# A chunked scan that feeds a two-layer network: ten scan units ahead of the first network step, six more by twos inside the first steps

## The chip, the core and the metric

The kernel runs on one core of one Trainium2 chip. The metric is device microseconds of that core. TensorE (PE in the profile, with PEld for its weight loads), VectorE (DVE), ScalarE (ACT), GpSimd (POOL) and the queue of transfers (SP) each work through a list of instructions of their own, in order; semaphores tie them together.

## The reference

Attention-like state scan over 4 batches and 8 heads, 768 tokens of 32 values, state of 16 rows, then a network over all 3072 tokens (256 to 2048 to 256, leaky ReLU):

```python
for c in range(nc):                      # chunks of 32 tokens
    xc, Bc, Cc = (x[:, :, sl], B[:, :, sl], C[:, :, sl])
    cum = np.cumsum(log_a[:, :, sl], axis=-1)
    L = np.exp(cum[:, :, :, None] - cum[:, :, None, :]) * causal
    CB = np.einsum('bhin,bhjn->bhij', Cc, Bc)
    y_intra = np.einsum('bhij,bhjd->bhid', CB * L, xc)
    y_inter = np.einsum('bhin,bhnd->bhid', Cc, state) * np.exp(cum)[..., None]
    y[:, :, sl] = y_intra + y_inter
    state = decay_full * state + sum_j(Bc * xc * decay_from_j)
h = y_as_tokens @ w_in                   # 3072 x 2048
out = np.maximum(0.01 * h, h) @ w_out    # 3072 x 256
```

The weights arrive in double precision; the kernel takes them as pairs of 32-bit words.

## The kernel before

**Units.** The scan is cut into 8 chunks of 96 tokens, each with 4 batches: 32 units of 8 heads, numbered 0 to 31 (four units a chunk). The state rides along as 16 extra rows of each tile, so a unit's tiles have 112 rows. A unit goes through these parts. Its *decay* is a tile of 112 x 768 named `lt`: for the early units a matmul of stacked sums (`decay_pe`, line 257, operands `dl` and `dr`, which `decay_load` brings from DRAM in slots) and an exp on ScalarE (`decay_of`, line 268); for units from 16 on, rows loaded by a transfer (`decay_rows`), a subtraction on GpSimd, an exp, a causal select on GpSimd. Its *scores* are eight small matmuls into a PSUM score tile, which VectorE multiplies into `lt` in two halves (`scores`, lines 313 and 318). Its *output* (`unit_out`: `unit_products`, lines 337 and 346, then `unit_halves`) is eight matmuls for the values and eight for the state; ScalarE copies the state (`stage`) and the values (`xh`, the rounded upper part), GpSimd puts the state into the next chunk's tile in four copies (line 373), and VectorE forms the remainder `xl` (line 380, the function `rest`). `pair_block` (line 400 and 412) does this for two units at a time: the outputs of two finished ones and the scores of two new ones share two score tiles.

**Steps.** The network works on 512-token tiles. For tiles 0 to 3 a step is one tile t and one block f of 128 hidden values: `ffn_in` (line 537, six matmuls, the in-half: upper and lower parts of operands, two K halves), two activations on ScalarE (`gh` and, by `ffn_act`, in place), the remainder `gl` on VectorE (`ffn_low`), and three steps later `ffn_out` (line 561, six matmuls, the out-half). `CELLS` orders the 64 steps: each entry is a tile and a range of blocks, and after each cell its output is copied or added into `ob`. Tile 0 needs units 0 to 5, tile 1 units to 10, tile 2 units to 15. Tiles 4 and 5 are done together at the end by another scheme, which nothing here touches.

**Weights.** Each of 16 blocks is decoded to single precision by passes: absolute value on ScalarE, then on VectorE hold, shift, sign and low (lines 433, 439, 446, 453), a cast to the upper part on ScalarE (`wh`, line 459) and the subtraction for the lower part (`wl`, line 466 on VectorE, or line 500 on GpSimd for the blocks in `POOLED`). `decode(n)` records the next n passes; `defer` and `settle` record the ScalarE and GpSimd operations that follow a pass at a later place.

**Order.** Nothing reorders the work: each engine's list is the order in which the program text records it. Before, sixteen units run one by one ahead of the steps (`FIRST_UNITS`), with the first step's in-half inside the last of them; the running sums for the later units (`columns`, `sum_rows`) follow the scores of unit 15, in the same score tile. From step 8 on, `PAIR` says at which step two new units get their scores.

**PSUM.** `ps_c` holds two score tiles, `ps_d` two tiles for decays and outputs ahead of the steps; after these, the banks of `ps_d` become `ps_o` (two output banks) and `ps_h` (two in-half banks). A new tile waits until the last reader of the old one in its place is done.

Of the kernel before, what the change touches and what calls it, by code (L numbers as in the profile page):

```python
# [18 lines left out]
Q = 96  # L19
NC = S // Q  # L20
QE = Q + N
# [16 lines left out]
    (0, 0, 3), (1, 0, 3), (2, 0, 3), (0, 3, 7), (1, 3, 7), (2, 3, 7),  # L38
    (0, 7, 11), (1, 7, 11), (2, 7, 11), (0, 11, 16), (1, 11, 16), (2, 11, 16), (3, 0, 16),
# [21 lines left out]
def scan_ffn(ctx: ExitStack, tc: tile.TileContext, a_l, b_l, c_l, bn_l, x_l, w_l, out_l):  # L61
# [192 lines left out]
    def decay_pe(u, space):  # L254
# [49 lines left out]
    def scores(u, warm=0, sums=False):  # L304
        c, b = divmod(u, NB)
        lt = lts[u].rearrange("p (g h) i -> p g (h i)", h=2)
        for half in range(2):
# [11 lines left out]
            if half and sums:  # L319
                columns(ccol, upto, AF.Copy, sc[:, 0, 2 * Q:])  # L320
                prow = sc[:, 1, 2 * Q:4 * Q].rearrange("p (g i) -> p g i", g=2)
                for g in range(2):
                    sum_rows(prow[:, g], g)
                nc.scalar.copy(crow, prow)
                nc.sync.dma_start(crow_d.rearrange("(g p) i -> p g i", g=2), crow)
# [254 lines left out]
    with tc.tile_pool(name="ps_d", bufs=2, space=PSUM, reuse_waits="tile") as ps_d:  # L580
# [364 lines left out]
```

## Time and profile before

| | |
|---|---|
| median of 3 runs | 332.81 us (332.06 to 333.81) |
| the profiled execution | 333.69 us, its span 332.0 us |
| transfers | 26.29 MB in 11722 packets |
| granted TensorE clock, mean | 0.992 |

In the profile a row of a timeline gives the start, the duration, the engine, the line, the operation with output and inputs, and in brackets the idle time before it with what ended that wait. A row of groups gives count, busy time, mean of one in ns, and the idle time before. Times are from the start of the span.

### The profile page before, as it was taken

What the parts mean: (1) busy time and instruction counts of PE and PEld (TensorE: products, weight loads), DVE (VectorE), ACT (ScalarE), POOL (GpSimd) and SP (SyncE); (2) the same over time, 40 slices, a digit from 0 to 9 for tenths busy, and PEclk for the clock granted to TensorE, in tenths of its full rate; (3) what the DMA queues carried; (4) which work ended last, traced back from release to release, by engine and by line L of the source; (5) the groups of instructions that cost most, each with busy time, mean ns of one, the idle gap of its engine ahead of it and who ended that gap; (6) DMA issues with size and microseconds to landing.
All of it is one profiled execution on the core that took longest, in us unless ns stands there. A gap on an engine that the chain in (4) does not pass through costs nothing.

```text
span 332.0 us, 6283 instructions
## 1 busy us (share of the span) xinstructions
PE 316.9 (95%) x2407; PEld 246.6 (74%) x2407; DVE 217.4 (65%) x351; ACT 182.2 (55%) x354; POOL 124.6 (38%) x214
## 2 busy tenths in 40 slices
PE   8879889899989999999999999999999999999995
PEld 4446567678868887778888878788876787778774
DVE  5879829996897988783432534167367767657651
ACT  4667637755656475644454443466355556555551
POOL 6258821522342444442323550051034565336100
PEclk9999979999999999999999999999999999999999
DMA  6886605393422812042211301000001000000003
GB/s 183 248 225 184 224 12 168 104 233 109 138 74 85 254 63 85 0 149 63 85 64 29 123 0 65 0 0 2 0 0 63 2 0 0 2 0 2 0 2 126
DMA packets 11722, 26.29 MB, mean 79 GB/s; under 512 B 2380, under 2 KB 4652, under 8 KB 11692
## 3 DMA queue, kind: packets, MB, share of 16 engines
q1 hardware_dynamic: 11692, 25.89, 25.5%
q8 instruction: 19, 0.31, 0.4%
q14 instruction: 11, 0.09, 0.1%
HBM read 22.57 MB, written 3.32 MB: 78 GB/s over the span
## 4 chain that ended last, share of the span: by engine, by line
PE 78%; DVE 9%; ACT 3%; issue 3%; ACTq 0%; DVEq 0%
PE op L561 24%; PE hp L537 22%; PE sc L761 9%; PE sc L780 6%; PE op L780 4%; PE hp L761 3%; PE sc L400 2%; PE sc L313 2%; DVE u L841 2%; DVE c L842 2%; PE sc L337 2%; PE pd L337 2%; PE pd L257 1%; DVE w L446 1%; PE pd L537 1%
## 5 line engine op out<-in xcount | busy, mean ns | idle before, releaser
L550 DVE TENSOR_TENSOR gl<-hp,gh 128x512 fp32r<-128x512 f32 x62 | 42.6, 687 | 58.7 <-ACT hp L547 58.5
L544 ACT ACTIVATE gh<-hp 128x512 fp32r<-128x512 f32 x62 | 37.0, 596 | 67.2 <-PE hp L537 67.1
L561 PE MATMUL op<-gh,wh 128*128 128x512 f32 x128 | 50.9, 398 | 2.7 <-DVE ob L575 1.3
L561 PE MATMUL op<-gh,wl 128*128 128x512 f32 x128 | 49.9, 390 | 0.0
L561 PE MATMUL op<-gl,wh 128*128 128x512 f32 x128 | 49.9, 389 | 0.0
L537 PE MATMUL hp<-xh,wh 128*128 128x512 f32 x124 | 48.7, 393 | 0.1
L537 PE MATMUL hp<-xh,wl 128*128 128x512 f32 x124 | 48.3, 389 | 0.0
L537 PE MATMUL hp<-xl,wh 128*128 128x512 f32 x124 | 48.3, 389 | 0.0
L373 POOL COPY xs<-stage 16x64 f32<-16x64 f32 x112 | 28.6, 256 | 42.3 <-ACT stage L370 35.3
L727 POOL TENSOR_TENSOR sl<-s,sh 128x512 fp32r<-128x512 f32 x8 | 10.4, 1298 | 73.1 <-ACT sh L726 73.1
L547 ACT ACTIVATE hp<-hp 128x512 f32<-128x512 f32 x62 | 36.8, 593 | 0.0
L289 POOL TENSOR_SCALAR_AFFINE_SELECT lt<-lt 96x768 f32<-96x768 f32 x16 | 14.6, 915 | 53.5 <-ACT lt L288 47.5
L561 PEld LDWEIGHTS op<-gh,wh 128*128 128x128 f32 x128 | 24.0, 188 | 10.1 <-DVE ob L575 1.7
L280 POOL TENSOR_TENSOR lt<-lt,ccol 112x768 f32<-112x768 f32 x16 | 24.3, 1520 | 13.8 <-DMA lt<-crow_d 9.6
L537 PEld LDWEIGHTS hp<-xh,wh 128*128 128x128 f32 x124 | 23.3, 188 | 6.2 <-DVE gl L550 1.1
L561 PEld LDWEIGHTS op<-gl,wh 128*128 128x128 f32 x128 | 24.0, 188 | 5.1
L561 PEld LDWEIGHTS op<-gh,wl 128*128 128x128 f32 x128 | 24.0, 188 | 4.7
L537 PEld LDWEIGHTS hp<-xl,wh 128*128 128x128 f32 x124 | 23.3, 188 | 4.9
L537 PEld LDWEIGHTS hp<-xh,wl 128*128 128x128 f32 x124 | 23.3, 188 | 4.7
L793 DVE TENSOR_TENSOR gl<-c,gh 128x512 fp32r<-128x512 f32 x24 | 24.4, 1038 | 1.4 <-ACT c L790 1.2
L789 ACT ACTIVATE gh<-c 128x512 fp32r<-128x512 f32 x24 | 15.0, 626 | 14.6 <-DVE c L842 9.1
L412 DVE TENSOR_TENSOR lt<-sc,lt 112x384 f32<-112x384 f32 x32 | 15.6, 548 | 3.3 <-ACT xh L375 1.9
(164 smaller groups left out, 629.2 us busy)
## 6 DMA issues: line engine op xcount, KB each, us to landing
raw<-w_l SPq DMA_DIRECT2D x16, 512.0 KB, 3.6
lt<-crow_d SPq DMA_DIRECT2D x16, 336.0 KB, 4.9
xs<-x_l SPq DMA_DIRECT2D x8, 384.0 KB, 5.2
out_l<-ob SPq DMA_DIRECT2D x12, 256.0 KB, 2.0
bn<-bn_l SPq DMA_DIRECT2D x8, 231.0 KB, 6.2
bt<-b_l SPq DMA_DIRECT2D x8, 224.0 KB, 3.3
cc<-c_l SPq DMA_DIRECT2D x16, 96.0 KB, 3.3
la<-a_l SPq DMA_DIRECT2D x1, 96.0 KB
```

The costliest lines, as they stand in the source:

```text
L280: nc.gpsimd.tensor_tensor(out=lts[u], in0=lts[u], in1=ccol[:, u * NH:(u + 1) * NH].unsqueeze(2).to_broadcast([QE, NH, Q]), op=ALU.subtract,)
L373: nc.gpsimd.tensor_copy(to[:, :, hh], stage[hh * D:hh * D + N])
L412: nc.vector.tensor_tensor(out=heads, in0=spaces[half][:QE, :, 2 * Q * e:2 * Q * (e + 1)], in1=heads, op=ALU.mult,)
L537: nc.tensor.matmul(hp, lhsT=w_half[half][:, f, k * 128:(k + 1) * 128], rhs=x[t][:, k, :], start=(n == 0), stop=(n == 5),)
L544: nc.scalar.activation(ghs[s], hp, AF.Prelu, alpha=0.01)
L547: nc.scalar.activation(hps[s], hps[s], AF.Prelu, alpha=0.01)
L550: nc.vector.tensor_tensor(out=gls[s], in0=hps.pop(s), in1=ghs[s], op=ALU.subtract)
L561: nc.tensor.matmul(op, lhsT=w_half[half][:, f, DM + m * 128:DM + (m + 1) * 128], rhs=x, start=(first and i == 0), stop=(last and i == 2),)
L761: nc.tensor.matmul(bank, lhsT=w[h], rhs=x[g], start=start and i == 0, stop=i == 2, skip_group_check=True,)
L780: nc.tensor.matmul(outs[t][m], lhsT=w_half[half][:, f, DM + m * 128:DM + (m + 1) * 128], rhs=x, start=first and i == 0, stop=last and i == 2,)
L789: nc.scalar.activation(gh, h, AF.Prelu, alpha=0.01)
L793: nc.vector.tensor_tensor(out=gl, in0=g, in1=gh, op=ALU.subtract)
```

## The change

`FIRST_UNITS` goes from 16 to 10. In the last of these ten, after the decay of unit 11, the scores of units 10 and 11 are taken together, then the first step's in-half, then unit 9's output. Step 0 takes the outputs of 10 and 11 with the scores of 12 and 13, step 2 the outputs of 12 and 13 with the scores of 14 and 15, step 4 the outputs of 14 and 15. The decays of units 12 to 15 use the stacked operands, one in a spare PSUM tile right behind the pair, the other after the next step's in-half; the multiplications of the two units stand in the following step, one on each side of that step's `ffn_low`. The running sums go into the spare tile in step 2. The spare tile holds the output banks' place until step 3; outputs of steps 0 and 1 follow in step 4. The cells have 2, 4 and 4 blocks at first. Blocks 0 to 3 instead of 1 and 2 are subtracted on GpSimd. The decode passes ahead of the steps are spread differently, the absolute value of a block follows the low pass of the one before it, a slot copy moves up, and two transfers (x of the third chunk, weight block 2) are issued later.

```diff
--- before.py
+++ after.py
@@ -35,23 +35,27 @@
 CELLS = (
-    (0, 0, 3), (1, 0, 3), (2, 0, 3), (0, 3, 7), (1, 3, 7), (2, 3, 7),
-    (0, 7, 11), (1, 7, 11), (2, 7, 11), (0, 11, 16), (1, 11, 16), (2, 11, 16), (3, 0, 16),
+    (0, 0, 2), (1, 0, 4), (2, 0, 4), (0, 2, 7), (1, 4, 8), (2, 4, 8),
+    (0, 7, 12), (1, 8, 12), (2, 8, 12), (0, 12, 16), (1, 12, 16), (2, 12, 16), (3, 0, 16),
 )
...
-FIRST_UNITS = 16
-POOLED = (1, 2)
-AHEAD = 2
+FIRST_UNITS = 10
+STACKED = 16
+POOLED = (0, 1, 2, 3)
...
-PAIR = {16: 8, 18: 14, 20: 20, 22: 26, 24: 32, 26: 38, 28: 44, 30: 49}
+STACKED_AT = {12: 0, 14: 2}
+STACKED_OUT = 4
+SUMS_AT = 2
+HELD_OUT = 3
+PAIR = {16: 10, 18: 15, 20: 20, 22: 26, 24: 32, 26: 38, 28: 44, 30: 49}
...
-PASSES = (3, 3)
+PASSES = 2
...
-            if half and sums:
-                columns(ccol, upto, AF.Copy, sc[:, 0, 2 * Q:])
...
+    def late_sums(space):
+        pcol = space[:QE, 0, :ncols]
+        prow = space[:, 1, :2 * Q].rearrange("p (g i) -> p g i", g=2)
+        nc.tensor.matmul(pcol, lhsT=upto, rhs=la, start=True, stop=True)
+        for g in range(2):
+            sum_rows(prow[:, g], g)
+        nc.scalar.copy(ccol, pcol)
+        nc.scalar.copy(crow, prow)
+        nc.sync.dma_start(crow_d.rearrange("(g p) i -> p g i", g=2), crow)
...
-        for half in range(2):
-            for e, u in enumerate(new):
-                lt = lts[u].rearrange("p (g h) i -> p g (h i)", h=2)
+
+        def mults(e):
+            lt = lts[new[e]].rearrange("p (g h) i -> p g (h i)", h=2)
+            for half in range(2):
...
+        return rests, mults
+
+    def pair_now(done, new):
+        rests, mults = pair_block(done, new)
+        for e in range(len(new)):
+            mults(e)
         for rest in rests:
             rest()
...
     def do_sign(f):
         decode_sign(f)
-        defer(decode_abs, f + 1)
...
         defer(decode_high, f)
+        defer(decode_abs, f + 1)
...
         fill_slots(1, SLOTS // 2)
+        fill_slots(SLOTS // 2, SLOTS)
...
         fetch_w(1)
-        fetch_x(2)
         scores(0)
...
         for u in range(FIRST_UNITS):
-            if u == FIRST_UNITS - 1:
-                settle()
-                leads.close()
-                pg = ctx.enter_context(tc.tile_pool(name="pg", bufs=LAG + 2))
-                pob = ctx.enter_context(tc.tile_pool(name="pob", bufs=3))
-                ffn_in(0, free_tile()[:, 0])
-                ffn_act(0)
-                ffn_low(0)
...
             if u + 1 < FIRST_UNITS:
-                scores(u + 1, int(0 < u < 4), u + 2 == FIRST_UNITS)
+                scores(u + 1, int(0 < u < 4))
+            else:
+                pair_now((), (u + 1, u + 2))
+                settle()
+                pg = ctx.enter_context(tc.tile_pool(name="pg", bufs=LAG + 2))
+                ffn_in(0, free_tile()[:, 0])
...
+            if u == 3:
+                fetch_x(2)
+            if u == 4:
+                fetch_w(2)
...
-            if u == 0:
-                decode(2)
-                fill_slots(SLOTS // 2, SLOTS)
             if u:
                 settle(late=True)
-            if u > 1 and u < 11:
-                decode(1)
-        ffn_in(1, score_tile()[:, 0])
-
-    ps_o = ctx.enter_context(tc.tile_pool(name="ps_o", bufs=2, space=PSUM, reuse_waits="tile"))
+                if u != 3:
+                    decode(1)
+        ffn_act(0)
+        ffn_low(0)
+
     ps_h = ctx.enter_context(tc.tile_pool(name="ps_h", bufs=2, space=PSUM, reuse_waits="tile"))
+    spaces = ctx.enter_context(ExitStack())
+    ps_x = spaces.enter_context(tc.tile_pool(name="ps_x", bufs=1, space=PSUM, reuse_waits="tile"))
+    ps_o = None
+
+    def open_outs_pool():
+        nonlocal ps_o, pob
+        spaces.close()
+        leads.close()
...
+    def spare_tile():
+        return ps_x.tile([128, 2, TS], F32, name="px_")
...
     for s in range(total):
...
-        if s >= AHEAD:
+        if s:
             ffn_in(s)
+        if late:
+            decay_pe(late[0], spare_tile())
+        if s == SUMS_AT:
+            late_sums(spare_tile())
         if s:
             ffn_act(s)
         settle()
+        if late:
+            late[1](0)
         if s:
             ffn_low(s)
+        if late:
+            late[1](1)
+        late = None
+        if s in stacked_at:
+            u = stacked_at[s]
+            rests, mults = pair_block((u - 2, u - 1), (u, u + 1))
+            decay_pe(u, spare_tile())
+            for rest in rests:
+                rest()
+            late = (u + 1, mults)
         if s in pair_at:
-            pair_block(*pair_at[s])
-        decode(n)
+            pair_now(*pair_at[s])
+        decode(PASSES)
...
-        if rested or not outs_due or steps[outs_due[0]] not in firsts or outs_due[0] == 0:
+        if s == HELD_OUT:
+            open_outs_pool()
+        elif rested or not outs_due or steps[outs_due[0]] not in firsts or outs_due[0] == 0:
```

On ScalarE, ahead of the steps, from the exp of unit 4 on (`lt` exp, `stage` and `xh` copies; `w32` is a weight block's absolute value, `wh` its upper part). Before:

```order
L268 ACTIVATE lt_307<-pd_304 112x768
L370 COPY stage_335<-pd_318 128x64
L375 CAST xh_237<-pd_318 128x2x96
L428 ACTIVATE w32_350<-raw_203 128x512
L459 CAST wh_150<-w32_194 128x512
L268 ACTIVATE lt_357<-pd_354 112x768
L370 COPY stage_387<-pd_370 128x64
L375 CAST xh_237<-pd_370 128x2x96
L268 ACTIVATE lt_401<-pd_398 112x768
```

With the change:

```order
L272 ACTIVATE lt_305<-pd_302 112x768
L377 COPY stage_333<-pd_316 128x64
L382 CAST xh_237<-pd_316 128x2x96
L272 ACTIVATE lt_350<-pd_347 112x768
L377 COPY stage_380<-pd_363 128x64
L382 CAST xh_237<-pd_363 128x2x96
L272 ACTIVATE lt_394<-pd_391 112x768
L377 COPY stage_421<-pd_404 128x64
L382 CAST xh_237<-pd_404 128x2x96
L472 CAST wh_150<-w32_195 128x512
L441 ACTIVATE w32_435<-raw_204 128x512
L272 ACTIVATE lt_441<-pd_438 112x768
```

The absolute value of block 1 and the cast of block 0 moved from ahead of the exp of unit 5 (`lt_357`) to behind the exp of unit 6 and the copies of unit 4.

On VectorE, the last unit ahead of the steps and steps 0 and 1 (L322 and L420 multiply scores into `lt`, L387 forms `xl`, L563 `gl`, the others are decode passes). Before, from the multiplication of unit 15:

```order
L318 TENSOR_TENSOR lt_792<-sc_827,lt_792 112x384
L318 TENSOR_TENSOR lt_792<-sc_831,lt_792 112x384
L380 TENSOR_TENSOR xl_688<-pd_841,xh_687 128x2x96
L550 TENSOR_TENSOR gl_881<-pd_873,gh_880 128x512
L380 TENSOR_TENSOR xl_688<-pd_885,xh_687 128x2x96
L433 TENSOR_SCALAR w32_747<-w32_747 128x512
L439 TENSOR_SCALAR w32_747<-w32_747 128x512
L446 SCALAR_TENSOR_TENSOR w32_747<-raw_611,w32_747 128x512
L550 TENSOR_TENSOR gl_918<-sc_910,gh_917 128x512
L453 SCALAR_TENSOR_TENSOR w32_747<-raw_611,w32_747 128x512
L433 TENSOR_SCALAR w32_931<-w32_931 128x512
```

With the change, from the low part of unit 11:

```order
L387 TENSOR_TENSOR xl_726<-sc_684,xh_725 128x2x96
L459 SCALAR_TENSOR_TENSOR w32_610<-raw_431,w32_610 128x512
L466 SCALAR_TENSOR_TENSOR w32_610<-raw_431,w32_610 128x512
L420 TENSOR_TENSOR lt_745<-sc_683,lt_745 112x384
L420 TENSOR_TENSOR lt_745<-sc_684,lt_745 112x384
L563 TENSOR_TENSOR gl_768<-hp_760,gh_767 128x512
L420 TENSOR_TENSOR lt_773<-sc_683,lt_773 112x384
L420 TENSOR_TENSOR lt_773<-sc_684,lt_773 112x384
L446 TENSOR_SCALAR w32_778<-w32_778 128x512
L452 TENSOR_SCALAR w32_778<-w32_778 128x512
```

Where before the low parts of steps were separated by decode passes only, the multiplications of units 12 and 13 now stand around the low part of step 1.

On TensorE, from behind the scores of units 14 and 15 at the end of step 2 into step 3, with the change (`px_` is the spare tile, `hp` the in-half's bank):

```order
L261 LDWEIGHTS dl_125
L261 MATMUL px__864<-dr_126,dl_125 112x384
L261 LDWEIGHTS dl_125
L261 MATMUL px__864<-dr_126,dl_125 112x384
L550 MATMUL hp_875<-xh_468,wh_150 128x512
L550 MATMUL hp_875<-xh_468,wl_151 128x512
L550 MATMUL hp_875<-xl_469,wh_150 128x512
L550 MATMUL hp_875<-xh_468,wh_150 128x512
L550 MATMUL hp_875<-xh_468,wl_151 128x512
L550 MATMUL hp_875<-xl_469,wh_150 128x512
L261 LDWEIGHTS dl_125
L261 MATMUL px__885<-dr_126,dl_125 112x384
```

The two decays stand on either side of an in-half, each in the spare tile; before, no decay stands between steps at this place.

More of the change, by code (lines that the diff above doesn't have):

```diff
@@ L262, in decay_pe @@
         after_u = u + SLOTS - LOAD + 1
-        if (u - DIRECT + 1) % LOAD == 0 and after_u < FIRST_UNITS:
-            decay_load(after_u, min(LOAD, FIRST_UNITS - after_u))
+        if (u - DIRECT + 1) % LOAD == 0 and after_u < STACKED:
+            decay_load(after_u, min(LOAD, STACKED - after_u))
     def decay_of(u, space):
@@ L300, in state_decay, with scores @@
         )
-    def scores(u, warm=0, sums=False):
+    def scores(u, warm=0):
         c, b = divmod(u, NB)
@@ L318, in scores @@
             nc.vector.tensor_tensor(out=heads, in0=sc[:QE, :, :2 * Q], in1=heads, op=ALU.mult)
-            if half and sums:
-                columns(ccol, upto, AF.Copy, sc[:, 0, 2 * Q:])
[L321 to L325, printed above, removed]
+    def late_sums(space):
[7 more added lines that the diff above has]
+        nc.sync.dma_start(crow_d.rearrange("(g p) i -> p g i", g=2), crow)
     xh, xl, x32 = {}, {}, {}
@@ L624, in scan_ffn @@
         for u in range(FIRST_UNITS):
-            if u == FIRST_UNITS - 1:
-                settle()
-                leads.close()
-                pg = ctx.enter_context(tc.tile_pool(name="pg", bufs=LAG + 2))
-                pob = ctx.enter_context(tc.tile_pool(name="pob", bufs=3))
-                ffn_in(0, free_tile()[:, 0])
-                ffn_act(0)
-                ffn_low(0)
             v = u + 2
-            if 0 < u and v < FIRST_UNITS:
+            if u:
                 decay_pe(v, free_tile())
@@ L645, in scan_ffn @@
                 decay_pe(v, pd)
-            rest()
             c, b = divmod(u, NB)
-            if c + 2 <= FIRST_UNITS // NB:
+            if c + 2 <= 3:
                 if b == 0 and c:
@@ L653, in scan_ffn @@
                     fetch_bc(c + 2)
-                    if c == 0:
-                        fetch_w(2)
                 if b == 3:
                     fetch_bn(c + 2)
-            if b == 2 and c + 1 < FIRST_UNITS // NB:
+            if u == 3:
+                fetch_x(2)
+            if u == 4:
+                fetch_w(2)
+            if b == 2 and c < 2:
                 state_decay(c + 1)
@@ L661, in scan_ffn @@
                 fetch_more()
-            if u == 0:
-                decode(2)
-                fill_slots(SLOTS // 2, SLOTS)
             if u:
                 settle(late=True)
-            if u > 1 and u < 11:
-                decode(1)
-        ffn_in(1, score_tile()[:, 0])
-    ps_o = ctx.enter_context(tc.tile_pool(name="ps_o", bufs=2, space=PSUM, reuse_waits="tile"))
+                if u != 3:
+                    decode(1)
+        ffn_act(0)
+        ffn_low(0)
     ps_h = ctx.enter_context(tc.tile_pool(name="ps_h", bufs=2, space=PSUM, reuse_waits="tile"))
+    spaces = ctx.enter_context(ExitStack())
[5 more added lines that the diff above has]
+        leads.close()
+        pob = ctx.enter_context(tc.tile_pool(name="pob", bufs=3))
+        ps_o = ctx.enter_context(
+            tc.tile_pool(name="ps_o", bufs=2, space=PSUM, reuse_waits="tile")
+        )
+    def spare_tile():
+        return ps_x.tile([128, 2, TS], F32, name="px_")
     early = {}
@@ L687, in scan_ffn @@
     pair_at[LAST_OUT] = ((NU - 2, NU - 1), ())
-    for c in range(FIRST_UNITS // NB, NC):
+    pair_at[STACKED_OUT] = ((STACKED - 2, STACKED - 1), ())
+    at(early, 0, state_decay, 3)
+    at(early, 1, alloc_x, 4)
+    at(early, 1, fetch_x, 4)
+    at(early, 1, fetch_bc, 4)
+    at(early, 2, fetch_bn, 4)
+    for c in range(STACKED // NB, NC):
         b = PAIR[NB * c]
-        if NB * c > FIRST_UNITS:
+        if NB * c > STACKED:
             b0 = PAIR[NB * (c - 1)]
@@ L867, in scan_ffn @@
     combining, rhs = None, {}
-    outs_due, rested = collections.deque(), False
+    outs_due, rested, late = collections.deque(), False, None
+    stacked_at = {s: u for u, s in STACKED_AT.items()}
     for s in range(total):
```

5 lines of the change are left out of this document (3 added, 2 removed).

## The prediction

> **What bounds the kernel now.** I read the page first, then busy time by stretch, then the timelines of the engines in the stretch that the change rewrites. The profiled execution took 333.69 us, its span 332.0, so 1.69 lie around the span; the median of the runs shown is 332.81, 0.88 below the profiled one.
>
> ```profile
> PE 316.9 (95%) x2407; PEld 246.6 (74%) x2407; DVE 217.4 (65%) x351; ACT 182.2 (55%) x354; POOL 124.6 (38%) x214
> 0.00:30.19 30.19, 26.03 (x417) 15.35 (x417) 22.73 (x56) 18.59 (x40) 16.59 (x47) 1.00 0.72 206
> 30.19:59.49 29.30, 26.62 (x341) 19.22 (x341) 20.80 (x42) 17.67 (x43) 13.76 (x37) 0.94 0.47 151
> 59.49:332.00 272.51, 264.30 (x1651) 212.06 (x1649) 173.90 (x255) 145.93 (x274) 94.26 (x130) 1.00 0.19 57
> ```
>
> After the page's first line the columns are the stretch, its length, then busy time of PE, PEld, DVE, ACT and POOL, the granted clock, the DMA share and GB/s. From 59.49 us on, PE is busy in 264.3 of 272.5 us, and only less matmul work or fewer waits help there. Ahead of it PE is called busy too, but the timeline shows short matmuls that wait for the other engines:
>
> ```profile
> 20.73 0.48 PE L257 MATMUL pd<-dr,dl 123*112 123x384 bf16 x2 [2.01 <-ACT lt L268]
> 30.19 0.86 PE L313 MATMUL sc<-cc,bt 32*112 32x192 f32 x8
> 30.98 0.54 PE L337 MATMUL pd<-lt,xs 112*32 112x96 f32 x16
> 31.57 0.53 PE L257 MATMUL pd<-dr,dl 123*112 123x384 bf16 x2
> 32.03 0.59 PE L313 MATMUL sc<-cc,bt 32*112 32x192 f32 x8
> 42.12 0.69 PE L209 MATMUL sc<-la,upto 96*112 96x256 f32 x2 [0.98 <-DVE lt L318]
> 43.28 0.85 PE L213 MATMUL sc<-upto,la 96*128 96x96 f32 x4 [0.47 <-ACT ccol L210]
> 45.08 0.80 PE L537 MATMUL pd<-xh,wh 128*128 128x512 f32 x1
> 59.49 0.39 PE L537 MATMUL hp<-xh,wh 128*128 128x512 f32 x1
> ```
>
> The scores of unit 10 start at 30.19, those of unit 11 at 32.03: 1.84 us per unit. The first step's matmuls start at 45.08. By 59.49 PE has done the in-halves of six steps and the out-halves of three: nine half steps. So 30.19 to 59.49, 29.30 us, holds the scores of units 10 to 15, the outputs of units 9 to 15, the running sums and nine half steps.
>
> Later, where units go by twos between steps, the chain of waits prices the same work:
>
> ```profile
> 84.08 1.36 PE hp L537 x6
> 86.48 0.86 PE sc L400 x16
> 87.35 1.58 PE op L561 x6
> ```
>
> A half step is 1.36. The first pieces leave 85.44 to 86.48 for the products of two units, 1.04, then 0.86 for the scores of two; the next half step takes 0.22 more than usual. That is 1.90 for two units plus 0.22, against 2 x 1.84 for two units ahead of the steps.
>
> **The lead, units 0 to 9.** Two things move here. The weight block's second half of decoding (ACT's absolute value and cast) leaves its place before the decay of unit 5:
>
> ```profile
> 18.79 0.66 ACT L428 ACTIVATE w<-raw 128x512 f32<-128x512 f32 x1 [1.36 <-DMA raw<-w_l]
> 19.36 0.60 ACT L459 CAST wh<-w 128x512 fp32r<-128x512 f32 x1
> 19.86 0.81 ACT L268 ACTIVATE lt<-pd 112x768 f32<-112x768 f32 x1
> 8.94 1.02 DVE L318 TENSOR_TENSOR lt<-sc,lt 112x384 f32<-112x384 f32 x2 [1.13 <-ACT lt L268]
> 12.48 0.68 DVE L446 SCALAR_TENSOR_TENSOR w<-raw,w 128x512 uint32<-128x512 uint32 x1
> 13.20 0.69 DVE L453 SCALAR_TENSOR_TENSOR w<-raw,w 128x512 uint32<-128x512 uint32 x1
> 13.81 0.95 DVE L183 COPY dr<-dr 120x3072 bf16<-120x3072 bf16 x1
> ```
>
> ACT stood 1.36 us for the raw block, then did both operations, and only at 19.86 the exp for which PE waited 2.01 us at 20.73. In the change both stand two exps later; the block has landed by then (18.79 in this trace, with one more transfer of 384 KB around it), so the 2.01 go. The slot copy of 0.95 moves into DVE's gap of 1.13 before 8.94, where it is hidden; at its old place, 13.81, the multiplication of unit 2 followed it. The two decode operations ahead of it (12.48 and 13.20) return one unit later each, so not all of this is won; I take 0.4 of the 0.95. **Lead: 2.4**, with ends at 1.36 (the DMA wait alone) and 3.0 (2.01 and 0.95). The moved transfer of x for the third chunk, now issued at unit 3 rather than at unit 0, needs to land by unit 8's products some 8 us later; POOL's new subtraction for weight block 0 stands before unit 5's state copies, which are first read four units on.
>
> **The stretch from unit 10 to the ninth half step.** On PE the change needs: nine half steps, 9 x 1.36 = 12.24; three pairs of scores, 3 x 0.86 = 2.58; three pairs of products, 3 x 1.04 = 3.12; unit 9's output, 31.57 - 30.98 = 0.59; four decays (12 to 15) at 32.03 - 31.57 = 0.46, 1.84; the sums, 0.69 + 0.85 = 1.54; three slower restarts, 0.66. Sum 22.57. (It has seven in-halves and two out-halves where the kernel before has six and three, by the hold-back of outputs until step 4.)
>
> Then the waits. Products of a pair write into a score tile, which is free once DVE has multiplied both earlier units' scores out of it. The second unit's multiplications now stand behind a decode pass pair, the first unit's and the step's low half:
>
> ```profile
> L318 DVE TENSOR_TENSOR lt<-sc,lt 112x384 f32<-112x384 f32 x32 | 16.2, 547 | 1.7 <-ACT lt L268 1.1 <-PE sc L313 0.5
> L550 DVE TENSOR_TENSOR gl<-hp,gh 128x512 fp32r<-128x512 f32 x62 | 42.6, 687 | 58.7 <-ACT hp L547 58.5
> L446 DVE SCALAR_TENSOR_TENSOR w<-raw,w 128x512 uint32<-128x512 uint32 x16 | 12.6, 785 | 0.0
> L453 DVE SCALAR_TENSOR_TENSOR w<-raw,w 128x512 uint32<-128x512 uint32 x16 | 15.8, 990 | 0.2
> L380 DVE TENSOR_TENSOR xl<-pd,xh 128x192 fp32r<-128x192 f32 x14 | 4.9, 352 | 5.3 <-ACT xh L375 5.2
> L375 ACT CAST xh<-pd 128x192 fp32r<-128x192 f32 x14 | 4.6, 326 | 0.0
> L370 ACT COPY stage<-pd 128x64 f32<-128x64 f32 x16 | 3.4, 212 | 7.6 <-PE pd L346 7.2 <-POOL xs L373 0.3
> ```
>
> Let P be the end of a pair's scores on PE. ACT's two copies of the first unit, 0.21 + 0.33 = 0.54, let DVE start. Steps 0 to 2: DVE then has three low pieces (3 x 0.35 = 1.05), sign and low passes (0.79 + 0.99), two multiplications (1.02, the pair at 8.94), the low half (0.69), two more (1.02): 5.56, done at P + 6.1. PE meanwhile has decay, in-half, decay, in-half, sums: 0.46 + 1.36 + 0.46 + 1.36 + 1.54 = 5.18, and some 0.3 for the spare tile, whose next writer waits for its last reader. PE waits about 0.6. Steps 2 to 4 have no sums, 3.64 on PE, against 0.7 + 1.78 + 1.02 + 0.69 + 1.02 = 5.21 on DVE, done at P + 5.75: PE waits about 2.1 before the products of units 14 and 15. With 0.1 before the first pair, the waits are 2.8 and the stretch 25.4. **Gain 29.3 - 25.4 = 3.9.** What is queued behind that wait on PE is the out-halves of steps 0 and 1, held for it anyway, and in-half 5. If DVE's passes took 0.68 each as at 12.48 and 13.20, each wait would lose 0.4 and the gain be 4.7; with no wait at all 6.7, which DVE's work excludes. The other end is contention with POOL:
>
> ```profile
> 60.87 2.80 DVE L453 SCALAR_TENSOR_TENSOR w<-raw,w 128x512 uint32<-128x512 uint32 x1
> 60.81 0.87 POOL L289 TENSOR_SCALAR_AFFINE_SELECT lt<-lt 96x768 f32<-96x768 f32 x1 [1.72 <-ACT lt L288]
> 61.65 1.47 POOL L280 TENSOR_TENSOR lt<-lt,ccol 112x768 f32<-112x768 f32 x1
> 64.33 0.50 PE L561 MATMUL op<-gh,wh 128*128 128x512 f32 x1 [1.27 <-DVE ob L575]
> ...
> 25.00 0.69 DVE L446 SCALAR_TENSOR_TENSOR w<-raw,w 128x512 uint32<-128x512 uint32 x1
> 24.36 1.42 POOL L373 COPY xs<-stage 16x64 f32<-16x64 f32 x4 [0.15 <-ACT stage L370]
> ```
>
> A pass of 0.69 took 2.80 while POOL ran two operations of 2.34 together: 2.1 lost. Once in each of the two DVE chains, 4.2, and the gain of 3.9 is gone. I keep the means, which hold the contention of an average pass, because POOL's work in these steps is mostly state copies, four per unit, and beside those a pass took its usual 0.69 (25.00).
>
> [...]
>
> **The first change of cells.** [...] In the change the first copies stand in step 4, ahead of the first pair by decay rows (step 10, POOL's work from step 7), with two in-halves to cover them. That wait goes, but the next cell ends in step 8, amid POOL's work; I take half, **0.6**, ends 0 and 1.27.
>
> The decode count stays 16 blocks; every block is finished before the step that needs it, and PE, at 264.3 of 272.5, remains the bound behind. The number of cells is unchanged, so the output additions are too.
>
> **Sum.** 2.4 + 3.9 + 0.6 = 6.9: 333.69 - 6.9 = 326.8 for an execution like the profiled one, 325.9 against the median.
>
> **Rivals.** *POOL's lock in both chains.* For it: the 2.80 above. Against: the 0.69 beside state copies. Price 4.2: 325.9 + 4.2 = 330.1.
>
> *The clock falls again.*
>
> ```profile
> 41.00:42.00 1.00, 0.14 (x2) 0.00 (x0) 1.00 (x3) 0.00 (x0) 0.85 (x4) 1.00 0.00 0
> 42.00:43.00 1.00, 0.69 (x2) 0.27 (x2) 0.07 (x1) 0.16 (x1) 0.37 (x2) 1.00 0.00 0
> 44.00:45.00 1.00, 1.00 (x33) 0.94 (x32) 0.00 (x0) 0.32 (x1) 0.00 (x0) 0.50 0.00 0
> 46.00:47.00 1.00, 1.00 (x4) 0.71 (x4) 0.09 (x1) 0.00 (x0) 0.51 (x3) 0.50 0.00 0
> ```
>
> Two thinly used microseconds, then half clock for some three, costing about 1.5 of the 29.30. My sum has full clock. A wait of 2.1 before units 14 and 15 may bring this back: 325.9 + 1.5 = 327.4. Against: PE was empty for 2.01 at 20.73 and kept its clock. [...]
>
> *No difference.* The lead is set by data: x of the third chunk or the second weight block lands late at its new place and PE stands at unit 8 or 10 for what the lead gains (2.4), and the lock takes its 4.2 as well: 325.9 + 6.6 = 332.5.
>
> *Slower.* The spare tile is one buffer, used five times in steps 0 to 3 and each time written only after its last reader; PE runs in order, so in-halves queue behind it. I count 0.3. An exp (0.81) behind both a step's activation and a cast (0.60 each) would cost 2.0 each time, 10 in all: 325.9 + 9.7 = 335.6. It decides from (6.9 + 0.3) / 5 = 1.4 per use. Against: the in-half of 1.36 lies between a tile's exp and its next writer.
>
> **How the numbers follow.** The forecast has 0.60, the clock 0.12, the lock 0.15, no difference 0.08, slower 0.05. Best ends, 3.0 + 4.7 + 1.27 = 9.0, give 332.8 - 9.0 = 323.8; I go to 323, since PE's 8.2 idle us behind 59.49 (272.51 - 264.30) may shrink a little as well. The upper end is the lock's with 0.4 for an unlucky lead, 330.5. About 0.5%, 1.7 us, can be told from no change. Faster by more (under 331.1): the forecast, the clock and most of the lock's, 0.86; within: 0.09; slower: 0.05.
>
> **What would show it.** The first in-half about 16 us earlier, near 29; no wait for the raw block before unit 5's exp; PE waits of some 0.6 and 2.1 before the products of units 12/13 and 14/15; the ninth half step ended near 53.2; later stretches the same length as before within a microsecond. Wrong if PE waits in step 1 or 3 for the spare tile by over 1 us, if DVE passes of 2 us stand in steps 0 to 4, or if what is gained by 60 us is lost by 130.

## The result and the profile after

The changed kernel took 323.78 us (median of four executions, 323.30 to 324.69), the kernel before 333.11 beside it: ratio 0.9726, 95% interval 0.969 to 0.9762. That is 9.3 us faster; the forecast was 6.9. Beside the later experiments, on two chips, the kernel before took 334.8 to 334.9 and the changed one 324.14 (ratio 0.9729, 0.9651 to 0.9808) and 324.29 (0.9698, 0.966 to 0.9735). The profiled execution took 324.14, its span 322.4 (332.0 before). First the page's line of engines, then busy time by stretch, cut where the prediction cut it:

```profile
PE 311.1 (96%) x2407; PEld 244.9 (76%) x2407; DVE 213.4 (66%) x349; ACT 181.4 (56%) x354; POOL 132.5 (41%) x216
0.00:27.57 27.57, 25.16 (x418) 14.91 (x418) 21.79 (x54) 17.83 (x38) 18.28 (x48) 1.00 0.74 224
27.57:51.60 24.03, 22.01 (x342) 17.86 (x341) 19.15 (x41) 17.26 (x43) 17.44 (x39) 1.00 0.59 187
51.60:322.40 270.80, 263.88 (x1651) 212.18 (x1649) 172.49 (x256) 146.33 (x275) 96.81 (x130) 1.00 0.18 58
```

The lead ends 30.19 - 27.57 = 2.62 us earlier. The stretch from unit 10 to the ninth half step takes 24.03 instead of 29.30, 5.27 less, at a granted clock of 1.00 where it had 0.94. What lies behind takes 1.71 less. The three make the 9.6 us between the spans.

PE's timeline in the new stretch (one row of each group; the multiplications are waited for in brackets):

```profile
21.62 0.48 PE L261 MATMUL pd<-dr,dl 123*112 123x384 bf16 x2 [0.76 <-ACT lt L272]
...
27.57 1.37 PE L407 MATMUL sc<-cc,bt 32*112 32x192 f32 x16
28.86 0.50 PE L550 MATMUL pd<-xh,wh 128*128 128x512 f32 x1
30.45 0.54 PE L344 MATMUL pd<-lt,xs 112*32 112x96 f32 x16
31.95 0.93 PE L407 MATMUL sc<-cc,bt 32*112 32x192 f32 x16
33.05 0.48 PE L261 MATMUL px__742<-dr,dl 123*112 123x384 bf16 x2 [0.17 <-DVE gl L563]
33.24 0.53 PE L550 MATMUL hp<-xh,wh 128*128 128x512 f32 x1
34.75 0.49 PE L261 MATMUL px__770<-dr,dl 123*112 123x384 bf16 x2
34.94 0.53 PE L550 MATMUL hp<-xh,wh 128*128 128x512 f32 x1
36.46 0.60 PE L327 MATMUL px__799<-la,upto 96*112 96x256 f32 x2
36.90 0.58 PE L217 MATMUL px__799<-upto,la 96*128 96x96 f32 x4
37.97 0.54 PE L344 MATMUL sc<-lt,xs 112*32 112x96 f32 x16 [0.50 <-DVE lt L420]
...
44.86 0.54 PE L344 MATMUL sc<-lt,xs 112*32 112x96 f32 x16 [1.36 <-DVE lt L420]
46.01 0.50 PE L574 MATMUL op<-gh,wh 128*128 128x512 f32 x1
51.60 0.39 PE L574 MATMUL op<-gh,wh 128*128 128x512 f32 x1
```

The first in-half starts at 28.86, the ninth half step ends at 51.60. PE waits three times: 0.17 for the spare tile, then 0.50 and 1.36 for the multiplications of the pair before. VectorE's rows around the longer wait:

```profile
41.06 0.68 DVE L459 SCALAR_TENSOR_TENSOR w<-raw,w 128x512 uint32<-128x512 uint32 x1
41.78 0.69 DVE L466 SCALAR_TENSOR_TENSOR w<-raw,w 128x512 uint32<-128x512 uint32 x1
42.39 1.01 DVE L420 TENSOR_TENSOR lt<-sc,lt 112x384 f32<-112x384 f32 x2
43.65 0.69 DVE L563 TENSOR_TENSOR gl<-hp,gh 128x512 fp32r<-128x512 f32 x1 [0.24 <-ACT hp L560]
44.26 1.01 DVE L420 TENSOR_TENSOR lt<-sc,lt 112x384 f32<-112x384 f32 x2
```

It is the chain that the prediction laid out, in its order; the sign and low passes take 0.68 and 0.69.

### The profile page after: what moved, and what is told of

Read it like the earlier page. It is cut to its first block, busy times and chain, and to the rows that moved or that the text cites. A ratio compares the mean times of both kernels' runs of the same rounds, so it can differ in the third digit from the quotient of the medians.

```text
span 322.4 us, 6284 instructions
## 1 busy us (share of the span) xinstructions
PE 311.1 (96%) x2407; PEld 244.9 (76%) x2407; DVE 213.4 (66%) x349; ACT 181.4 (56%) x354; POOL 132.5 (41%) x216
## 4 chain that ended last, share of the span: by engine, by line
PE 83%; DVE 8%; ACT 3%; issue 3%; DMA 2%; SPq 0%; ACTq 0%
PE op L574 26%; PE hp L550 24%; PE sc L792 9%; PE sc L811 6%; PE op L811 4%; PE hp L792 3%; PE sc L407 3%; PE sc L344 3%; DVE c L873 2%; DVE u L872 2%; PE sc L317 1%; PE pd L344 1%; PE pd L261 1%; DMA raw<-w_l 1%; DVE gl L563 1%
## 5 line engine op out<-in xcount | busy, mean ns | idle before, releaser
L563 DVE TENSOR_TENSOR gl<-hp,gh 128x512 fp32r<-128x512 f32 x63 | 43.4, 689 | 58.6 <-ACT hp L560 58.3
L550 PE MATMUL hp<-xh,wh 128*128 128x512 f32 x126 | 49.8, 395 | 0.4 <-DVE gl L563 0.4
L550 PE MATMUL hp<-xh,wl 128*128 128x512 f32 x126 | 49.1, 389 | 0.0
L550 PE MATMUL hp<-xl,wh 128*128 128x512 f32 x126 | 49.0, 389 | 0.0
L380 POOL COPY xs<-stage 16x64 f32<-16x64 f32 x112 | 31.6, 282 | 31.4 <-ACT stage L377 26.9
L284 POOL TENSOR_TENSOR lt<-lt,ccol 112x768 f32<-112x768 f32 x16 | 25.9, 1620 | 3.4 <-DMA lt<-crow_d 2.7
L420 DVE TENSOR_TENSOR lt<-sc,lt 112x384 f32<-112x384 f32 x44 | 21.6, 549 | 3.0 <-ACT xh L382 1.9
```

The source lines that it names most:

```text
L284: nc.gpsimd.tensor_tensor(out=lts[u], in0=lts[u], in1=ccol[:, u * NH:(u + 1) * NH].unsqueeze(2).to_broadcast([QE, NH, Q]), op=ALU.subtract,)
L380: nc.gpsimd.tensor_copy(to[:, :, hh], stage[hh * D:hh * D + N])
L420: nc.vector.tensor_tensor(out=heads, in0=spaces[half][:QE, :, 2 * Q * e:2 * Q * (e + 1)], in1=heads, op=ALU.mult,)
L550: nc.tensor.matmul(hp, lhsT=w_half[half][:, f, k * 128:(k + 1) * 128], rhs=x[t][:, k, :], start=(n == 0), stop=(n == 5),)
L563: nc.vector.tensor_tensor(out=gls[s], in0=hps.pop(s), in1=ghs[s], op=ALU.subtract)
```

## The experiments

The question that the result leaves is which part brought what: the sum of three independent gains (lead, stretch, cells) gave 6.9, and a right total says nothing of its parts.

### The new lead alone

The kernel before with the lead's new order; sixteen units, cells and sums as they were.

```diff
         decode_sign(f)
-        defer(decode_abs, f + 1)
...
         defer(decode_high, f)
+        defer(decode_abs, f + 1)
...
         fill_slots(1, SLOTS // 2)
+        fill_slots(SLOTS // 2, SLOTS)
...
         fetch_w(1)
-        fetch_x(2)
...
+            if u == 3:
+                fetch_x(2)
+            if u == 4:
+                fetch_w(2)
...
-            if u > 1 and u < 11:
-                decode(1)
+                if u != 3 and u < 13:
+                    decode(1)
```

> The kernel before with the new lead alone: slot copy early, absolute value of a block behind the low pass of the one before, passes spread as in the change, x of the third chunk and weight block 2 issued later; sixteen units still run ahead, block subtractions and cells are the old ones. Theory (the terms add): the exp of unit 5 no longer waits behind the raw block, the scores of unit 10 start near 27.6 instead of 30.19, the time falls by 2.6 to about 330.5. Rival (the lead's gain is given back at the sums or at the first step, because the end of the lead waits for something else): 333, no difference.

Measured 334.22 beside 334.76, ratio 0.9982 (0.9946 to 1.0017): no difference. In the profiled execution the units carry the 2.2 us as far as the sums, and some of it is gone behind them:

```profile
27.95 1.05 PE L313 MATMUL sc<-cc,bt 32*112 32x192 f32 x8
36.40 1.04 PE L313 MATMUL sc<-cc,bt 32*112 32x192 f32 x8 [0.88 <-DVE lt L318]
38.21 1.04 PE L313 MATMUL sc<-cc,bt 32*112 32x192 f32 x8 [0.17 <-DVE lt L318]
40.00 1.20 PE L209 MATMUL sc<-la,upto 96*112 96x256 f32 x2 [0.75 <-DVE lt L318]
41.67 1.17 PE L213 MATMUL sc<-upto,la 96*128 96x96 f32 x4 [0.47 <-ACT ccol L210]
43.78 0.80 PE L537 MATMUL pd<-xh,wh 128*128 128x512 f32 x1
58.52 0.39 PE L537 MATMUL hp<-xh,wh 128*128 128x512 f32 x1
```

Unit 10 starts at 27.95 instead of 30.19, the sums at 40.00 instead of 42.12. On the way PE waits 0.88, 0.17 and 0.75 for the multiplications (0.98 in all before); the kernel before has a wait of 0.95 at 33.96 instead, for nothing that its profile shows. Then the sums take 1.20 and 1.17 instead of 0.69 and 0.85: the granted clock was 0.50 from 40 to 46 us, about twice as long as in the kernel before. The first in-half is 1.30 us earlier than before, the end of the ninth half step, at 58.52, still 0.97. Over ten executions even this is not seen in the time; why is not shown.

### The running sums alone

The kernel before with the sums in step 2, in a score tile.

```diff
...
-                scores(u + 1, int(0 < u < 4), u + 2 == FIRST_UNITS)
+                scores(u + 1, int(0 < u < 4))
...
+        if s == 2:
+            late_sums(score_tile())
```

> The kernel before with the running sums alone moved, from behind the scores of unit 15 to step 2, in a score tile. Theory: in the trace of before the sums with their waits keep TensorE from 41.1 to 44.06, and the half clock from 44 to 47 follows from these thin microseconds; moved, they cost 1.0, the clock stays full, and the time falls by about 3.3 to 329.8. Rival (the clock falls anyway, the units' chain sets the end of the lead): at most the two waits of 0.98 and 0.47, with 1.0 added later, about 332.5.

Measured 330.96, ratio 0.9876 (0.9813 to 0.9938): 4.1 us by the ratio, where the theory had 3.3. At their old place the sums had two waits, 0.98 and 0.47, and in the profiled execution stood on the edge of the half clock (1.00 in the window from 42 us, 0.83 in the one from 43, 0.50 in the one from 44); in step 2 they take 0.59 and 0.58 without a wait. The other half of the theory did not come: the clock did not stay full. The four executions have mean clocks of 0.983 to 0.999, and the profiled one stood at half clock for 6.8 us from 21.6 on, behind a wait of 1.9 for the exp of unit 5. What makes up the rest of the 4.1 is open.

### Lead and sums together: as run, the sums alone again

Both edits above were to stand in one kernel. The kernel that ran holds the edit of the sums only; its lead is the old one, and it is the kernel of the section before, line for line:

```diff
...
-                scores(u + 1, int(0 < u < 4), u + 2 == FIRST_UNITS)
+                scores(u + 1, int(0 < u < 4))
...
+        if s == 2:
+            late_sums(score_tile())
```

> The kernel before with two parts of the change: the new order of the lead and the running sums moved out of the last lead unit into step 2. Theory: the lead's 2.6 us were given back only because the running sums at the end of the lead ran in order behind thin work at half clock; with the sums elsewhere the two gains add up, 2.6 + 4.1 = 6.7, about 328. Rival: the lead's gain is lost in any case while units 10 to 15 stand ahead of the steps, since VectorE's multiplications set their pace (waits of 0.88 before units 13 to 15 were seen); then it stays at 331, as with the sums alone.

Measured 329.79 beside 334.89, ratio 0.9883 (0.9813 to 0.9953), on another chip than the 0.9876. That is one kernel measured twice. The wait for the exp of unit 5, which the new lead takes away, stands in its profile:

```profile
21.00 0.48 PE L257 MATMUL pd<-dr,dl 123*112 123x384 bf16 x2 [2.25 <-ACT lt L268]
```

So neither the theory nor the rival was tested: no run here has sixteen units, the moved sums and the new lead.

### The change without its lead

```diff
         decode_sign(f)
+        defer(decode_abs, f + 1)
...
         defer(decode_high, f)
-        defer(decode_abs, f + 1)
...
         fill_slots(1, SLOTS // 2)
-        fill_slots(SLOTS // 2, SLOTS)
...
         fetch_w(1)
+        fetch_x(2)
...
-                if u != 3:
-                    decode(1)
+            if 1 < u < 8:
+                decode(1)
```

> The changed kernel with the old lead: slot copy, passes, absolute value and the two transfers in their old places; ten units ahead, pairs, cells and GpSimd's four subtractions as changed. Theory (the terms add): the scores of units 10 and 11 start near 30.2 instead of 27.57, the rest keeps its length, the time rises by 2.6 to about 326.4. Rival (the pairs in the steps have slack that hides a late lead): 324, no difference.

Measured 327.82, ratio 0.9773 (0.9722 to 0.9824): some 3.5 us more than the changed kernel's 324.29 (measured on the same chip in a later comparison, with the kernel before within 0.2 us of the same time). Here the lead counts. PE's wait for the exp of unit 5 is back, and the first pair starts 30.93 - 27.57 = 3.36 us later:

```profile
20.41 0.48 PE L261 MATMUL pd<-dr,dl 123*112 123x384 bf16 x2 [1.70 <-ACT lt L272]
30.93 0.97 PE L407 MATMUL sc<-cc,bt 32*112 32x192 f32 x16
```

Behind that wait half clock stood for 3.4 us from 21.8 on, and the four executions have mean clocks of 0.987 to 0.995, the changed kernel's 0.997 or more. So a part of the 3.5 us is half clock, and not the order of the lead by itself.

### The change without its cells

```diff
-    (0, 0, 2), (1, 0, 4), (2, 0, 4), (0, 2, 7), (1, 4, 8), (2, 4, 8),
-    (0, 7, 12), (1, 8, 12), (2, 8, 12), (0, 12, 16), (1, 12, 16), (2, 12, 16), (3, 0, 16),
+    (0, 0, 3), (1, 0, 3), (2, 0, 3), (0, 3, 7), (1, 3, 7), (2, 3, 7),
+    (0, 7, 11), (1, 7, 11), (2, 7, 11), (0, 11, 16), (1, 11, 16), (2, 11, 16), (3, 0, 16),
```

> The changed kernel with the cells of before (three blocks in each of the first three cells). Theory: step 2 now wants block 2, whose lower part is done at 38.68 in the trace of the change, while the in-half of step 2 starts at 34.94; TensorE waits up to 3.7, of which the later waits of 0.50 and 1.36 take back some; the time rises by 2 to 3.7, about 326.5. Rival (the cells make no difference, the decode has slack): 324.

Measured 331.09, ratio 0.9894 (0.9857 to 0.993): 6.8 us over the changed kernel's 324.29, twice what was expected, and no better than the sums alone. PE's longest waits in the steps, beside the 1.36 for the multiplications:

```profile
38.17 0.49 PE L550 MATMUL hp<-xh,wh 128*128 128x512 f32 x1 [2.07 <-ACT wh L472]
39.58 0.50 PE L550 MATMUL hp<-xh,wl 128*128 128x512 f32 x1 [0.92 <-POOL wl L512]
76.01 0.50 PE L550 MATMUL hp<-xh,wl 128*128 128x512 f32 x1 [1.23 <-DVE wl L479]
93.56 0.47 PE L574 MATMUL op<-gh,wh 128*128 128x512 f32 x1 [1.74 <-ACT w L441]
```

Three of the four are for decoded weights: the upper part of block 2 (2.07) and its lower part (0.92), both in step 2, and a later lower part (1.23). With cells of 3 blocks step 2 is tile 0 with block 2; with a first cell of 2 it is tile 1 with block 0, decoded long before, and block 2 is wanted at step 4. After the two waits in step 2 half clock stood for 3.4 us from 40.5 on.

### The cells without the units by twos

The kernel of the two sections on the sums (sixteen units, sums moved, the old lead, not the new one that the expectation speaks of) with the cells of the change.

```diff
-    (0, 0, 3), (1, 0, 3), (2, 0, 3), (0, 3, 7), (1, 3, 7), (2, 3, 7),
-    (0, 7, 11), (1, 7, 11), (2, 7, 11), (0, 11, 16), (1, 11, 16), (2, 11, 16), (3, 0, 16),
+    (0, 0, 2), (1, 0, 4), (2, 0, 4), (0, 2, 7), (1, 4, 8), (2, 4, 8),
+    (0, 7, 12), (1, 8, 12), (2, 8, 12), (0, 12, 16), (1, 12, 16), (2, 12, 16), (3, 0, 16),
```

> The kernel before with the new lead, the sums in step 2 and the cells of the change; units 10 to 15 still stand ahead of the steps. Theory: the cells are worth 6 to 7 us only where the units by twos push the decoding of weight blocks into the steps, because cells of 2, 4 blocks ask for block 2 at step 4 instead of step 2; here the blocks were decoded ahead of the steps, so the cells bring nothing but the wait of 1.27 us for the first output copy: 328 to 330. Rival: the cells bring their 6 us whatever the units do, and the units by twos nothing: 323 to 324.

Measured 332.43 beside 334.88, ratio 0.9931 (0.989 to 0.9971): no gain over 0.9876 and 0.9883 without the cells, if anything a loss. The rival's 323 to 324 did not come, though the test was made with the old lead. The kernels with the sums moved make a table; the rows with ten units hold the change's other edits in the steps too:

| ratio to the kernel before | cells of 3, 3, 3 | cells of 2, 4, 4 |
|---|---|---|
| sixteen units ahead, one by one, old lead | 0.9876, 0.9883 | 0.9931 |
| ten ahead, six by twos in steps, old lead | not run | 0.9773 |
| ten ahead, six by twos in steps, new lead | 0.9894 | 0.9698 |

Beside the moved sums alone, the units by twos with the new lead bring nothing under the old cells, and the cells bring nothing under sixteen units. Units and cells together bring some 3.6 us, with the new lead some 6. Sixteen units with the new lead and the moved sums were not run with either cells. That it is the units, and not the new lead, that make the cells pay is therefore read from the profiles: PE waits for block 2 in step 2 with ten units and the old cells, and does not wait there in either profile of sixteen units, the moved sums and the old cells.

### Twelve units ahead

```diff
-FIRST_UNITS = 10
+FIRST_UNITS = 12
...
-STACKED_AT = {12: 0, 14: 2}
-STACKED_OUT = 4
+STACKED_AT = {14: 0}
+STACKED_OUT = 2
...
```

> The changed kernel with twelve units ahead of the steps and one pair (14 and 15) inside steps 0 to 2. Theory: the gain of the units by twos comes from spreading VectorE's multiplications and the decays over steps, so one pair fewer costs about a third of it, 1.3 us, 325.4. Rival: the gain is the moved sums and cells alone, and the number of units ahead of the steps does not matter: 324.

Measured 328.16, ratio 0.983 (0.977 to 0.989), which fits neither: the profile showed a wait that my edit had made.

```profile
37.86 0.33 PE L353 MATMUL sc<-xs,bn 112*32 112x32 f32 x16 [2.31 <-POOL bn L299]
```

GpSimd decayed the fourth chunk's state keys only in step 0, where with twelve units ahead they are first read. So once more, with that operation at unit 10:

```diff
-            if b == 2 and c < 2:
+            if b == 2:
                 state_decay(c + 1)
...
-    at(early, 0, state_decay, 3)
```

> Twelve units ahead and one pair in the steps, as before, but the decay of the fourth chunk's state keys is done on GpSimd at unit 10 and not in step 0, since the products of units 12 and 13 waited 2.31 us for it there. Theory: the kernel of twelve units was slow by that wait, and without it has a third of the gain of the units by twos less than the changed kernel, 325.4. Rival: the wait moves to another cause, since the second unit's multiplications are late anyway, and it stays at 328.

Measured 325.32, ratio 0.9736 (0.968 to 0.9792), as the theory said; but the interval overlaps the changed kernel's 0.9698 (0.966 to 0.9735), so that twelve is worse by 1 us is likely and not shown.

### The second unit's multiplications ahead of the low half

```diff
         if late:
             late[1](0)
+            decode(1)
+            late[1](1)
         if s:
             ffn_low(s)
         if late:
-            late[1](1)
+            decode(1)
         late = None
...
-        decode(PASSES)
+        if not late:
+            decode(PASSES)
```

> The changed kernel, but in steps 1 and 3 the second unit's score multiplications stand directly after one decode pass behind the first unit's, ahead of the step's low half; the other decode pass comes last. Theory: the waits of 0.50 us before the products of units 12/13 and 1.36 before those of 14/15 are DVE's order alone, so they shrink to about 0 and 0.6, and the time to 322.6. Rival: what is won before the products is lost again, because the low half and the decoded blocks 2 and 3 come later for the out-halves and in-halves behind; then the time stays at 324, and PE waits for wl or gl in steps 2 to 5.

> The changed kernel with the second unit's score multiplications moved ahead of the low half and the second decode pass in steps 1 and 3, a second time. Theory: DVE's order alone made the two waits and the wait for the output copy behind them, so it is 2 us or more under the changed kernel on this chip too, 321.3 to 322. Rival: the first look's 2.8 us between the two profiled executions was chance between executions (it had one of 326.2 as well), and the medians lie within 0.5 us of each other.

beside the changed kernel as it is:

> The changed kernel as it is, beside the next kernels on the same chip. All theories: 323 to 325 us, first step's in-half at 28.9 us, ninth half step ended at 51.6, no microsecond with a granted clock under 1. If the half clock of the kernel before comes to any thin stretch, it can appear here too, and then the time would be about 1.5 to 2 us longer.

> The changed kernel as it is, in five rounds beside the next kernels on the same chip: 323.3 to 324.7 us.

322.70 (0.9658, 0.957 to 0.9746) beside executions of 324.07, 324.14 and 327.03 of the changed kernel, whose ratio was 0.9729 (0.9651 to 0.9808); a fourth, profiled one took 615.65 and is left out: the matmuls of its first two in-halves took 0.61 to 0.97 us, where they took 0.39 to 0.53 in the profile of the result, at a granted clock given as 1.0; why is open. Then 322.94 (0.9654, 0.961 to 0.9697) beside 324.29 (0.9698). The medians differ by 1.4 us both times (the first time by 2.3 without the execution of 327.86), less than the 2 us that the second expectation asked for. The intervals overlap, and six of the ten executions lie under the lowest of the other's nine. Of the two waits one is gone and one is short:

```profile
37.56 0.54 PE L344 MATMUL sc<-lt,xs 112*32 112x96 f32 x16
43.38 0.54 PE L344 MATMUL sc<-lt,xs 112*32 112x96 f32 x16 [0.27 <-DVE lt L420]
```

So the order on VectorE made them, and this kernel, the fastest run here, probably beats the changed one; how firmly, these executions do not settle. The decoded blocks came in time all the same.

## Why the prediction was right, and where it was not

**The lead**, 2.4 forecast, measured 2.62, and the agreement is luck: two sizes missed in opposite ways. By the starts of the units' scores, 1.42 us are won by unit 4 (16.11 for 17.53), where 0.4 was counted for the slot copy. Unit 5 is 3.39 earlier (17.75 for 21.14), since its exp no longer waits behind a raw block. Unit 7 has 2.37 left (22.04 for 24.41): the two operations now stand ahead of the exp of unit 7, and PE waits 0.76 for that one. The prediction let all of the 2.01 go. Nor did it say that this term has no worth of its own: alone it brought nothing (0.9982), in the change 3.5 us, of which a part is half clock. It was written as one of three addends. Why it is worth nothing under sixteen units with the sums at their old place is open; in the one profile some of it was lost at half clock (6.84 us of it for 3.40 in the kernel before).

**The stretch**, 3.9 forecast, measured 5.27. Its length by the prediction's terms, from the starts of the rows above:

| term | forecast | measured |
|---|---|---|
| nine half steps with restarts | 12.90 | 13.39 |
| scores of three pairs | 2.58 | 3.09 |
| products of three pairs, unit 9 | 3.71 | 3.71 |
| four decays | 1.84 | 0.80 |
| sums | 1.54 | 1.01 |
| waits | 2.8 | 2.03 |
| sum | 25.4 | 24.03 |

Three sizes failed. A decay was taken as the start of the scores minus the start of the decay in the old lead, 0.46, which holds the lead's own pauses; between half steps it takes 34.94 - 34.75 = 0.19 by the starts, and some of its cost falls into the half step behind it. The sums were taken from rows that began at full clock and ended at half, 0.69 + 0.85; at full clock, from 36.46 to the end of the row at 36.90, 1.02. And the waits were taken with VectorE's mean passes (0.79 and 0.99), where the passes in these steps took 0.68 and 0.69; the bound for that case, 0.4 less per wait, was nearly what happened (0.50 and 1.36 for 0.6 and 2.1). Against this, the first scores of two at 27.57 took 1.29, and half steps after a decay 1.50 to 1.68. The sum also says nothing of what one part of it is worth without the others: the moved sums alone, a term of 1.54 in it, brought 4.1 us in the kernel of sixteen units.

**The first change of cells**, 0.6 forecast, failed as a step, though the total hid it. I priced the copy that frees the output tile, for which PE waits 1.27 at 64.33 in the kernel before; there the copy (63.59, 0.68, line 575) comes on VectorE right after the pass of 2.80 at 60.87. The 0.6 is half of that wait, an estimate that no run shows by itself. And I took the decoding as settled: "every block is finished before the step that needs it". That is true only through the cells. Without them the change loses 6.8 us, of which decoded weights that come late are 2.07 + 0.92 + 1.23 in the profile, and the half clock behind the first two a part; the rest was not followed up. Since this cost was absent in the changed kernel, leaving it out did the forecast no harm. The copy's wait itself did not vanish: 1.27 before, 1.05 now, at another place.

**Behind**, 270.80 for 272.51, 1.71 less where 0.6 was forecast, and more than the microsecond that the prediction allowed. PE's idle time fell from 8.21 to 6.92: a wait for a decoded block in the kernel before is not there any more:

```profile
95.55 0.47 PE L561 MATMUL op<-gh,wh 128*128 128x512 f32 x1 [1.18 <-ACT wh L459]
```

Part of this differs between executions of one kernel. In this one, a pass of 0.68 took 1.96 beside a subtraction on GpSimd, and the output's addition and PE stood behind it:

```profile
101.70 1.96 DVE L459 SCALAR_TENSOR_TENSOR w<-raw,w 128x512 uint32<-128x512 uint32 x1
103.59 1.27 DVE L582 TENSOR_TENSOR ob<-op,ob 128x512 f32<-128x512 f32 x2
101.32 1.79 POOL L284 TENSOR_TENSOR lt<-lt,ccol 112x768 f32<-112x768 f32 x1 [2.18 <-DMA lt<-crow_d]
104.41 0.47 PE L574 MATMUL op<-gh,wh 128*128 128x512 f32 x1 [1.05 <-DVE ob L582]
```

In another execution of the same kernel that pass took 0.68, and PE did not wait:

```profile
102.06 0.68 DVE L459 SCALAR_TENSOR_TENSOR w<-raw,w 128x512 uint32<-128x512 uint32 x1
```

In the first of the two GpSimd had waited 2.18 us for a transfer of rows. That the landing of this transfer decides where the subtraction meets VectorE's pass is an estimate; no row shows GpSimd in the other execution.

**The rivals.** *POOL's lock in both chains*, one pass in each chain lengthened beside GpSimd like the 2.80 at 60.87, did not come: no pass of 2 us in steps 0 to 4. GpSimd's work there, with one of VectorE's hold passes:

```profile
37.40 1.28 POOL L512 TENSOR_TENSOR wl<-w,wh 128x512 fp32r<-128x512 f32 x1 [0.40 <-ACT wh L472]
38.30 0.67 DVE L446 TENSOR_SCALAR w<-w 128x512 f32<-128x512 f32 x1
40.33 3.06 POOL L380 COPY xs<-stage 16x64 f32<-16x64 f32 x8 [1.64 <-ACT stage L377]
44.29 1.28 POOL L512 TENSOR_TENSOR wl<-w,wh 128x512 fp32r<-128x512 f32 x1 [0.90 <-ACT wh L472]
```

The passes at 41.06 and 41.78 ran beside state copies and took their usual 0.68 and 0.69. The subtractions of 1.28 fell beside multiplications (37.37 and 44.26), and neither was lengthened: the multiplications took 1.01 as at 42.39, the subtractions 1.28 for 1.30 at 29.64. The hold passes behind these multiplications, at 38.30 and 45.19, took 0.67 instead of the 0.42 at 99.58, beside the ends of the subtractions; PE did not wait for them. (Newly subtracted on GpSimd are blocks 0 and 3.) Why the pass at 101.70 took 1.96 beside a subtraction on GpSimd, and those beside the copies 0.68 and 0.69, is not shown. *The clock falls again* did not come either: thirteen executions of the changed kernel had a mean clock of 0.997 to 1.0, and what the profiled one lacks lies at its end (0.72 in the window from 321 us, 0.50 behind it), where TensorE has no work left (busy 0.00 from 320 us on). *Slower by the spare tile*: 0.17 us in all, against 0.3 counted and 1.4 per use needed. *No difference*: unit 8 did not stand for x.

## What to carry to other kernels

A right total is no evidence for its addends: take each part out of the change and put each in alone, since here ten units with the new lead brought nothing without the cells, the cells nothing with sixteen units, and all together 6 us. Look in the profile of each such kernel for the sign of the part that it should hold: the wait of 2.25 us that the new lead takes away told that one kernel here lacked it. When work moves from a lead into steps, list which decoded or loaded operand each step wants first and when it is ready; an order that asks for the next operand two steps later can be worth more than the work that was moved. Take an operation's duration from a place where its engine runs without pauses at full clock, not from the distance of two starts in a stretch that waits.

## What was not expected of the hardware

The half clock came in pieces of one length. Each stretch of it ahead of the span's end, summed from windows of 1 us (a window at 0.83 holds 0.34 us of half clock), was 3.4 or 6.8 us long in the seven profiles that show one. The kernel before, from 42 us on, and the change with the old cells:

```profile
43.00:44.00 1.00, 0.72 (x4) 0.62 (x4) 0.00 (x0) 0.22 (x1) 0.00 (x0) 0.83 0.00 0
45.00:46.00 1.00, 1.00 (x14) 0.84 (x5) 0.27 (x1) 0.43 (x2) 0.42 (x2) 0.50 0.36 98
47.00:48.00 1.00, 1.00 (x30) 0.63 (x32) 0.00 (x0) 0.32 (x1) 0.00 (x0) 0.97 0.00 0
```

```profile
40.00:41.00 1.00, 1.00 (x5) 0.81 (x4) 0.28 (x1) 0.00 (x0) 0.00 (x0) 0.73 0.07 19
42.00:43.00 1.00, 1.00 (x9) 0.82 (x11) 0.00 (x0) 0.00 (x0) 0.00 (x0) 0.50 0.00 0
43.00:44.00 1.00, 1.00 (x41) 1.00 (x44) 0.00 (x0) 0.95 (x3) 0.00 (x0) 0.56 0.00 0
```

0.34 + 3 + 0.06 = 3.40, and 0.54 + 2 + 0.88 = 3.42. In the kernel with the lead alone it was 0.40 + 6 + 0.44 = 6.84. One such piece lowers the mean clock of an execution by 1.7 / 332 = 0.005. The end of the span, when TensorE has no work left for it to slow, can lower it too: 1.6 us of it in the profile before, where TensorE is busy 0.00 from 329 us on, make 0.0024. The 42 executions of the kernel before fall into groups that fit this: 0.995 to 0.992 (18 of them), 0.990 to 0.987 (12), 0.985 to 0.982 (8), 0.979 to 0.977 (3) and 0.973 (1). Read so, they have one to five pieces, on average 2.0, and none is without. The medians of their spans are 331.95 us with one piece, 333.1 with two and 334.0 with three, so about 1 each; but spans with one piece run from 330.4 to 335.1. Some 2 us of what the change gains may be that it has none, a loose estimate from these medians. Half clock followed waits of PE of 1.70, 1.9, 2.07, 2.25 and 2.31 us in profiles of the kernels above, and two thin microseconds in the kernel before (PE busy 0.14 and 0.69 from 41 to 43 us), which had kept its clock of 1.00 after 2.01. In the kernel with the lead alone it came at 39.6, where no wait since 30 us had been longer than 0.88. So here the longest wait did not decide; in the changed kernel, which kept its clock, the longest inside the work is 1.36. What sets off a piece, and why one kernel has a different number of them each time, these runs do not tell.
